# A fused linear-attention and mixture-of-experts kernel: PSUM tiles split, late logits grouped, token lists ahead of gate weights, x stored in one transfer, expert weights loaded two steps later

## The chip, the cores and the metric

The kernel runs on one core of a Trainium2 chip. The core has five engines that run side by side and meet through semaphores: TensorE (PE: matrix products; its weight loads are listed apart as PEld), VectorE (DVE), ScalarE (ACT), GpSimd (POOL) and SyncE (SP, which here only issues transfers). Transfers between the chip's memory and SBUF, the core's working memory, are carried out by 16 DMA engines. PSUM is the memory that TensorE writes; it has 8 banks of 2 KB per partition.

The metric is the device time of one execution in microseconds (us); lower is better.

## The reference, cut to what matters

```python
# linear attention: batch 4, 8 heads, 768 positions, head size 48
state = zeros((B, H, D, D))
for t in range(S):
    cur = einsum('bhd,bhe->bhde', u[None] * k[:, :, t], v[:, :, t])
    y[:, :, t] = einsum('bhd,bhde->bhe', r[:, :, t], state + cur)
    state = w[None, :, :, None] * state + einsum('bhd,bhe->bhde', k[:, :, t], v[:, :, t])
x = y as 3072 tokens of 384 numbers

# experts: 8 experts, hidden size 1024
do_compute = x @ w_skip > 0
logits = x[do_compute] @ w_gate
e_idx = argmax(logits); gate_w = softmax(logits)[e_idx]
for e in range(8):
    mask = e_idx == e
    y[mask] = gate_w[mask] * (relu(x[mask] @ w1[e]) @ w2[e])
out = x;  out[do_compute] = x[do_compute] + y
```

Each token that passes the skip score is sent to one expert, and the expert's output, weighted, is added to the token. All data are 32-bit floats.

## The kernel before, in words

**Tiles.** The 3072 tokens are 24 tiles (`NT`) of 128: two pairs of batches, 12 blocks of 64 positions (`C`) each; a tile holds the same 64 positions of the two batches of a pair, one batch on partitions 0 to 63 and one on 64 to 127. The blocks of a pair are linked by the recurrent state, so they run in order.

**The recurrence (lines 853 to 896).** Step n of the loop works on tile n+1 and finishes tile n. In order, on TensorE: `scores` (L445, keys against queries, into `ps_p`), `turn_k` (L458, keys transposed), `across` (L527, the part of the output that comes from the state), `turn_x` (L565, tile n transposed), `state` (L478, the state's update, into `ps_s[:, 0]`), the logits of tile n (`gate`, L573) and `within` (L504, the part of the output from the block itself, for which VectorE's `mask_scores`, L466 and L467, must be done). `evac` (L538) copies the finished x tile from PSUM to SBUF, and `put_x` (L552) stores it to the output tensor by two transfers of 64 rows, one per batch. Tiles 12 to 15 are stored a second time, as tiles 16 to 23 in two halves each, into rows that are rewritten later (so that a first gather may read them before).

**Logits.** Up to tile 15 the logits are made for four tiles at once: `gate_four` (L591) loads the gate's weights once per tile into a quarter of the array and multiplies by the transposed x; ScalarE copies the result (L600), and a step later `gate_back` (L604, L605) transposes it back through `ps_s[:, 1]` and copies it into `lg`. From tile 16 on, each tile has its own `gate` (L573), in which the transposed x is the loaded operand.

**Routing.** `route(g0, g1)` turns the logits of a group of tiles (`GROUPS`: 0 to 8, 8 to 16, 16 to 20, 20 to 24) into lists: for each expert, in each of two halves (j = 0 up to 128 tokens, j = 1 the rest), which token stands at which place, and its gate weight in two parts. It is a generator: each `yield` ends a portion, and `step_route` and `tick` place the portions in the steps, a `yield 4` at one of two places of a step. Its PSUM is `ps_s[:, 1]` (for the last group `ps_l`): ranks are counted by matmuls (L652 to L662), and the lists are collected by matmuls (L722, L747) of a one-hot matrix `ol` with the values `vl`: token id and the two parts of the weight (`NV3` = 3). After tile 15, L754 reduces the counts, `place(0)` derives from the lists the gather's indices `gid`, the scatter's `sid` and the weights `gate_s`, and a first indirect gather fetches the first tokens of expert 0.

**Expert weights.** `load_piece` (L108) loads a piece of 256 KB (128 partitions of 512 numbers) on the SP queue; `split_piece` splits it into a high part (ScalarE, L113) and a low part (POOL or VectorE, L114), so that products keep their precision. There are 12 pieces per expert (`NPC`). In step n, piece n-2 is loaded at the end (`FIRST_LOAD` = 2), and piece n-4 is split in the middle (`LEAD` = 2), on ScalarE ahead of the copy of the transposed keys (L460). Three buffers (`NST`) hold raw pieces.

**Order.** The program fixes the order of every engine by the order of the lines; nothing is rearranged. SP issues, per step: dm (keys and queries, L271, 512 KB, five tiles ahead), vz (values, L279, two of 96 KB, four tiles ahead), the two x stores, and the raw piece. What reads or writes a tile of PSUM or SBUF waits for what touched the tile before it where the two accesses may collide.

**The passage and the experts (lines 902 to 1040).** `first` and `second` are generators (`single`) for the first and second 128 tokens of expert 0, run in pieces (`run`) between the routing of the last group. After `place(1)` the remaining gathers go out, then `PLAN`, a string that fixes the order of portions, finishes expert 0 and begins expert 1. Experts 1 to 7 then run in `expert`: `up` (L154), `rectify`, `down` (L164), `mix` (L169), `scatter` (L172). Their weights come by `load_next` through 14 buffers.

Of the kernel before, what the change touches and what calls it, by code (L numbers as in the profile page):

```python
# [22 lines left out]
P = 128  # L23
# [26 lines left out]
NST = 3  # L50
NST2 = 14
LEAD, FIRST_LOAD = 2, 2
# [7 lines left out]
def tile_wkv_moe(  # L60
# [18 lines left out]
    ps_s = psum.tile([P, 2, 512], F32, name="ps_s")  # L79
    ps_t, ps_l = (psum.tile([P, 512], F32, name=f"ps_{c}") for c in "tl")  # L80
# [163 lines left out]
    with ExitStack() as actx:  # L244
# [51 lines left out]
        nc.vector.memset(ps_s[:, 0, : 2 * NHP * D], 0.0)  # L296
# [172 lines left out]
        def state(n):  # L469
# [5 lines left out]
            s, nxt = ps_s[:, 0, : 2 * NHP * D].rearrange("p (q f) -> p q f", q=2), sblk[(n + 1) % 2]  # L475
# [72 lines left out]
        def put_x(n, x, parts=((0, 0), (1, 1))):  # L548
            pr, i = divmod(n, NSTEP)
            for to, b in parts:  # L550
                r0 = (NB * pr + to) * S + i * C
                ins = nc.sync.dma_start(out=out[r0 : r0 + C, :], in_=x[b * C : (b + 1) * C, :])  # L552
# [32 lines left out]
        def gate_four(n):  # L585
            four = [gts.pop(n - GB + 1 + j)[1] for j in range(GB)]
# [12 lines left out]
            lt = turned_lg[n] = wk.tile([P, P], F32, tag="lt", name=f"lt{n}", bufs=1)  # L599
            nc.scalar.copy(lt, pg)  # L600

        def gate_back(n):
            pb = ps_s[:, 1, 512 - P :]
            nc.tensor.transpose(pb, turned_lg.pop(n), ident)  # L604
            nc.scalar.copy(lg[:, n - GB + 1 : n + 1, :], pb.rearrange("p (j e) -> p j e", j=GB)[:, :, : E + 1])  # L605
            seen[0] = n
# [4 lines left out]
        def route(g0, g1):  # L611
            n, late = g1 - g0, g0 >= EARLY
            rp = ps_l if g1 == NT else ps_s[:, 1]
# [25 lines left out]
            if late:  # L639
                nc.scalar.activation(df, df, AF.Exp)  # L640
# [30 lines left out]
            nc.vector.tensor_reduce(gw, df, AX.X, ALU.add)  # L671
            nc.vector.tensor_scalar(gw, gw, 1e-9, None, ALU.add)
# [12 lines left out]
            if late:  # L685
                ranks()
                nc.vector.reciprocal(gw, gw)
                nc.vector.tensor_reduce(r1, rk, AX.X, ALU.add)
                nc.vector.tensor_copy(gh, gw)
# [16 lines left out]
            yield 0  # L706
# [3 lines left out]
            if late:  # L710
                nc.vector.tensor_tensor(
                    ol, lane1[:, None, :].to_broadcast([P, n, P]), r1.unsqueeze(2).to_broadcast([P, n, P]), ALU.is_equal
                )
                nc.vector.tensor_tensor(gl, gw, gh.bitcast(F32), ALU.subtract)
                vl = small("vl", F32R, NV3 * E)
                for q, val in enumerate(vals):
                    nc.vector.tensor_tensor(
                        vl[:, :, q * E : (q + 1) * E], oh, val.to_broadcast([P, n, E]), ALU.mult
                    )
                yield 4  # L720
                for j in range(n):
                    nc.tensor.matmul(  # L722
                        part[:, :, NJ - 1, :], ol[:, j, :], vl[:, j, :], start=(j == 0), stop=(j == n - 1)
                    )
                last = lists[:, :, NJ - 1, :]
                nc.vector.tensor_tensor(last, part[:, :, NJ - 1, :], last, ALU.add)
                count()
                nc.vector.tensor_tensor(before, before, sums, ALU.add)
# [24 lines left out]
            if g1 == EARLY:  # L753
                nc.tensor.matmul(pr[:, :E], ones[:, :P], before, start=True, stop=True)  # L754
                nc.vector.scalar_tensor_tensor(
                    before, pr[:, :E], float(P), ident[:, 0:1].to_broadcast([P, E]), ALU.max, ALU.mult
                )
                place(0)
                x_in.append(gather(0, wpool, x_out, (B - 1) * S + (EARLY - NSTEP) * C))

        def place(j):
            c = slice(j * E, (j + 1) * E)
            ids = lists[:, 0, j]
            nc.vector.tensor_scalar(gid[:, c], ids, 1.0, 0.0, ALU.subtract, ALU.max)
# [22 lines left out]
        def both(g):  # L787
# [4 lines left out]
            "ph": [ps_p[:, 0], ps_s[:, 1], ps_l, ps_y[:, 1]],  # L792
            "pt": [ps_s[:, 0], ps_t],
# [59 lines left out]
        for n in range(NT - 1):  # L853
# [5 lines left out]
            if 0 < n <= EARLY and n % GB == 0:  # L859
                gate_back(n - 1)  # L860
# [57 lines left out]
        run(2)  # L918
        both(last)
        place(1)  # L920
        order = [q for e in range(E) for q in (e, E + e)][1:]

    with ExitStack() as mctx:
        w2pool = mctx.enter_context(tc.tile_pool(name="w2pool", bufs=1, reuse_waits="tile"))
        rest = iter(order)
        for _ in range(NXG - 1):
            gather(next(rest), w2pool)
# [68 lines left out]
        split_next = splitter(1, done - NPC)  # L996
# [270 lines left out]
```

## Time and profile before

| | us |
|---|---|
| three runs, without a profile | 287.99 (median), 286.94, 289.4 |
| the profiled execution, its own time | 289.88 |
| its span, first to last instruction | 288.0 |
| mean granted TensorE clock in it | 0.97 of full |

How to read the views: the page's rows in 40 digits cut the span into 40 slices of 7.2 us; a digit is the busy share in tenths (for PEclk the granted clock). The timeline has the start (us), the duration (us), the engine, the line of the kernel, the operation, output and inputs, how many instructions were merged, and in brackets how long the engine had been idle before and what released it. In the groups by line the last columns are busy time in all and mean ns of one, then the idle time before them by releaser. The table by stage has, for each stretch, its length and each engine's busy time. The list of waits has total us, times, and the longest. A releaser is inferred; where a wait is for several things, the last one by the profile is named.

### The profile page before, as it was taken

The page shows a single profiled execution, that of the slowest core. Times are in us where ns is not written, and L with a number is a line of the kernel's source. Part 1 is how long each engine was busy: PE and PEld are TensorE (multiplying, and loading weights), DVE is VectorE, ACT ScalarE, POOL GpSimd, SP SyncE. Part 2 cuts the span into 40 slices and gives each one's busy share as a digit, 9 for nine tenths or more (in the row PEclk, how much of TensorE's full clock was granted, in tenths as well). Part 3 has the DMA queues.
Part 4 walks back from the last instruction along what each step waited for, and adds up shares of the span by engine and source line. Part 5 has one row for each costly group of instructions (what it writes and reads, how often), then busy time and mean ns, then how long its engine had stood idle before and what let it go on. Part 6 is the DMA issues. An engine that isn't in the chain of part 4 may idle for free.

```text
span 288.0 us, 9596 instructions
## 1 busy us (share of the span) xinstructions
PE 260.1 (90%) x3961; PEld 233.2 (81%) x3961; DVE 194.5 (68%) x370; ACT 141.1 (49%) x318; POOL 134.6 (47%) x135
## 2 busy tenths in 40 slices
PE   7869998885979998798969999999999999999991
PEld 2658776675767787687867999999999999999991
DVE  7837598699887899973624476796847659385210
ACT  2616565565556556545325453662817447282200
POOL 8464074555545535631084384564453534445111
PEclk9979999999979999979979999999999999999997
DMA  6956879769787878432358999467774847300000
GB/s 193 256 173 170 263 226 288 215 202 280 211 256 216 251 215 254 131 92 67 100 155 256 350 327 307 165 201 238 225 241 139 252 144 242 120 5 26 17 30 22
DMA packets 28134, 54.16 MB, mean 188 GB/s; under 512 B 4727, under 2 KB 11404, under 8 KB 28080
## 3 DMA queue, kind: packets, MB, share of 16 engines
q1 hardware_dynamic: 25744, 47.99, 54.6%
q0 software_dynamic: 2048, 5.44, 5.9%
q8 instruction: 33, 0.54, 0.8%
q14 instruction: 21, 0.17, 0.2%
q10 hardware_dynamic: 288, 0.02, 0.1%
HBM read 45.64 MB, written 8.65 MB: 188 GB/s over the span
## 4 chain that ended last, share of the span: by engine, by line
PE 66%; DMA 11%; DVE 7%; issue 6%; SPq 3%; ACT 3%; POOL 3%; POOLq 0%; ACTq 0%; DVEq 0%
PE ps_p L164 10%; PE ps_y L164 10%; DMA raw<-in_w_dram 8%; PE ps_p L154 5%; PE ps_y L154 5%; PE ps_s L154 5%; PE ps_l L154 5%; PE ps_p L445 5%; PE ps_s L478 4%; PE ps_y L504 4%; DMA dm<-in_dm_dram 2%; PE ps_y L527 2%; SPq L552 2%; PE ps_l L458 2%; PE ps_t L565 1%
## 5 line engine op out<-in xcount | busy, mean ns | idle before, releaser
L114 POOL TENSOR_TENSOR lo<-raw,hi 128x512 fp32r<-128x512 f32 x43 | 57.9, 1347 | 86.7 <-ACT hi L113 79.8
L113 ACT CAST hi<-raw 128x512 fp32r<-128x512 f32 x96 | 55.2, 623 | 12.5 <-DMA raw<-in_w_dram 12.5
L114 DVE TENSOR_TENSOR lo<-raw,hi 128x512 fp32r<-128x512 f32 x53 | 46.1, 891 | 2.7 <-ACT hi L113 1.9
L433 POOL TENSOR_TENSOR kd<-dm,w_d 128x512 f32<-128x512 f32 x22 | 32.3, 1468 | 6.7 <-DMA dm<-in_dm_dram 6.7
L172 POOL DMA_INDIRECT out_dram<-xg,sid x16 | 17.2, 1075 | 36.7 <-DVE xg L169 30.2
L445 PE MATMUL ps_p<-rd,kd 64*64 64x128 f32 x768 | 30.2, 290 | 3.1 <-issue 2.2
L466 DVE COPY_PREDICATED am<-below,ps_p 128x512 f32<-128x512 int8 x24 | 17.6, 732 | 18.4 <-PE ps_p L445 18.2
L445 PEld LDWEIGHTS ps_p<-rd,kd 64*64 64x64 f32 x768 | 24.0, 144 | 4.6 <-issue 3.2
L478 PE MATMUL ps_s<-vz,kt 128*64 128x96 f32 x352 | 19.9, 256 | 5.5 <-ACT kt L460 2.9
L478 PEld LDWEIGHTS ps_s<-vz,kt 128*64 128x64 f32 x352 | 15.7, 139 | 11.2 <-ACT kt L460 4.3
L122 POOL DMA_INDIRECT xg<-out_dram,gid x16 | 17.7, 1106 | 15.1 <-DVE gate_s L768 10.3
L415 DVE TENSOR_TENSOR rd<-dm,w_d 128x512 f32<-128x512 f32 x24 | 23.1, 962 | 1.1 <-DMA dm<-in_dm_dram 1.1
L158 ACT ACTIVATE hh<-ps_p 128x464 fp32r<-128x464 f32 x7 | 3.9, 559 | 37.8 <-PE ps_p L154 20.2
L504 PE MATMUL ps_y<-vz,am 64*64 64x48 f32 x768 | 17.8, 230 | 4.2 <-issue 2.5
L504 PEld LDWEIGHTS ps_y<-vz,am 64*64 64x64 f32 x768 | 14.5, 141 | 7.2 <-issue 3.4
L409 ACT ACTIVATE rd<-rd,uw 128x128 f32<-128x128 f32 x52 | 17.9, 397 | 4.5 <-DVE rd L415 4.5
L164 PE MATMUL ps_p<-hi,hh 128*128 128x384 f32 x56 | 19.4, 347 | 0.0
L164 PE MATMUL ps_y<-hi,hh 128*104 128x384 f32 x56 | 18.9, 338 | 0.0
L164 PE MATMUL ps_p<-hi,hl 128*128 128x384 f32 x56 | 18.9, 337 | 0.0
L164 PE MATMUL ps_y<-lo,hh 128*104 128x384 f32 x56 | 18.9, 337 | 0.0
L164 PE MATMUL ps_y<-hi,hl 128*104 128x384 f32 x56 | 18.9, 337 | 0.0
L164 PE MATMUL ps_p<-lo,hh 128*128 128x384 f32 x56 | 18.8, 336 | 0.0
(247 smaller groups left out, 682.5 us busy)
## 6 DMA issues: line engine op xcount, KB each, us to landing
raw<-in_w_dram SPq DMA_DIRECT2D x96, 256.0 KB
dm<-in_dm_dram SPq DMA_DIRECT2D x24, 512.0 KB
out_dram<-xt SPq DMA_DIRECT2D x56, 96.0 KB
vz<-in_tok_dram SPq DMA_DIRECT2D x48, 96.0 KB
xg<-out_dram,gid POOLq DMA_INDIRECT x16, 6.9
out_dram<-xg,sid POOLq DMA_INDIRECT x16, 2.7
w_in<-in_wd_dram SPq DMA_DIRECT2D x1, 8.0 KB
ub_sb<-in_ub_dram ACTq DMA_DIRECT2D x1, 2.0 KB
```

Source lines behind the costliest of these rows:

```text
L113: nc.scalar.copy(hi, t)
L114: eng.tensor_tensor(lo, t, hi.bitcast(F32), ALU.subtract)
L122: ins = nc.gpsimd.indirect_dma_start(out=xg, out_offset=None, in_=out[0:rows], in_offset=bass.IndirectOffsetOnAxis(ap=gid[:, q : q + 1], a ...
L154: nc.tensor.matmul(ph, a[:, c, fs], b[:, c, :], start=(k == 0), stop=(k == 3 * NCC - 1))
L164: nc.tensor.matmul(py, a, b[:, f, :], start=(k == 0), stop=(k == 3 * NFC - 1))
L409: nc.scalar.mul(rd[:, :, 1], rd[:, :, 0], uw[:, hp : hp + 1])
L415: nc.vector.tensor_tensor(rds[n][:, :, :, 0], d[:, 0], w_d[:, n % NSUB, 0][:, :, None].to_broadcast([DR, NHP, 2, C]), ALU.mult,)
L433: (eng or nc.gpsimd).tensor_tensor(kds[n], d[:, 1], w_d[:, n % NSUB, 1][:, :, None].to_broadcast([DR, NHP, 2, C]), ALU.mult,)
L445: nc.tensor.matmul(ps_p[q * C : (q + 1) * C, a, 2 * hp * C : 2 * (hp + 1) * C], kd[h, hp, q, :], rd[h, hp, q].rearrange("p s c -> p (s c)" ...
L466: nc.vector.copy_predicated(shape(am[n % 2]), below, p[:, :, 0])
L478: nc.tensor.matmul(s[a * C : (a + 1) * C, :, hp * D : (hp + 1) * D], kt[:, hp, a, :], t[:, :, a, hp, :], start=i == 0 and hp == 0, stop=Tr ...
L504: ins = nc.tensor.matmul(ps_y[b * C : (b + 1) * C, a, hp * D : (hp + 1) * D], am[n % 2][half, a, hp * C : (hp + 1) * C], t[half, q, a, hp, :],
```

## The change

Five edits go together.

1. The two-bank PSUM tile `ps_s` becomes two tiles, `ps_s` (state) and `ps_r` (routing). In the route that ends at tile 16 the matmul that reduces the counts stands ahead of the matmuls that collect the lists.
2. `gate_four` becomes `gate_some`: tiles 16 to 19 have their logits as a group of four, tiles 20 to 22 as a group of three; only tile 23 has a gate of its own.
3. In the late routes the token ids are collected by themselves and the gather's indices follow at once (`place_ids`); the gate weights are worked out and collected after that. At the end, the gather of expert 0's second tokens goes out before the weights are there.
4. An x tile is stored by one transfer of 128 rows, two blocks of 64 rows in the output, instead of two transfers; the second copy of tiles 12 to 15 likewise, as 128 rows in one block.
5. Weight pieces are loaded two steps later (`FIRST_LOAD` = 4), through four buffers (`NST` = 4), so two more are loaded and split after the loop.

The diff, with its smaller renamings left out:

```diff
-NST = 3
+NST = 4
-LEAD, FIRST_LOAD = 2, 2
+LEAD, FIRST_LOAD = 2, 4
...
-    ps_s = psum.tile([P, 2, 512], F32, name="ps_s")
-    ps_t, ps_l = (psum.tile([P, 512], F32, name=f"ps_{c}") for c in "tl")
+    ps_s, ps_r, ps_t, ps_l = (psum.tile([P, 512], F32, name=f"ps_{c}") for c in "srtl")
...
             if FIRST <= n < EARLY:
-                for b in range(NB):
-                    put_x(EARLY + NB * (n - FIRST) + b, x, ((0, b),))
-            put_x(n, x)
-
-        def put_x(n, x, parts=((0, 0), (1, 1))):
+                r0 = (B - NB) * S + (EARLY - NSTEP) * C + (n - FIRST) * P
+                put_x(n, x, out[r0 : r0 + P, :])
             pr, i = divmod(n, NSTEP)
-            for to, b in parts:
-                r0 = (NB * pr + to) * S + i * C
-                ins = nc.sync.dma_start(out=out[r0 : r0 + C, :], in_=x[b * C : (b + 1) * C, :])
-                if n >= EARLY:
-                    for other in x_in:
-                        tc.declare_no_dep(ins.ins, other, reason="the rows are disjoint")
-                    x_out.append(ins.ins)
+            put_x(n, x, out.rearrange("(b s) c -> b s c", b=B)[NB * pr : NB * (pr + 1), i * C : (i + 1) * C, :])
+
+        def put_x(n, x, to):
+            ins = nc.sync.dma_start(out=to, in_=x)
...
-        def gate_four(n):
-            four = [gts.pop(n - GB + 1 + j)[1] for j in range(GB)]
+        def gate_some(n, k=GB):
+            four = [gts.pop(n - k + 1 + j)[1] for j in range(k)]
...
+                def collect(v0, v1):
+                    for j in range(n):
+                        nc.tensor.matmul(
+                            part[:, v0:v1, NJ - 1, :],
+                            ol[:, j, :],
+                            vl[:, j, v0 * E : v1 * E],
+                            start=(j == 0),
+                            stop=(j == n - 1),
+                        )
+                    into = lists[:, v0:v1, NJ - 1, :]
+                    nc.vector.tensor_tensor(into, part[:, v0:v1, NJ - 1, :], into, ALU.add)
+
+                value(0)
+                yield 4
+                collect(0, 1)
+                if g1 == NT:
+                    place_ids(1)
+                yield 0
+                weigh()
+                nc.vector.reciprocal(gw, gw)
+                nc.vector.tensor_copy(gh, gw)
                 nc.vector.tensor_tensor(gl, gw, gh.bitcast(F32), ALU.subtract)
...
+                value(1, 2)
+                if g1 < NT:
+                    count()
+                    nc.vector.tensor_tensor(before, before, sums, ALU.add)
                 yield 4
...
+                collect(1, NV3)
...
             yield 2 if g1 < EARLY else 4
+            if g1 == EARLY:
+                nc.tensor.matmul(pr[:, :E], ones[:, :P], before, start=True, stop=True)
             for j in range(n):
                 nc.tensor.matmul(mine, ol[:, j, :], vl[:, j, :], start=(j == 0), stop=(j == n - 1))
...
-            if n >= EARLY:
-                gate(n)
-            elif n % GB == GB - 1:
-                gate_four(n)
+            if n < TE and n % GB == GB - 1:
+                gate_some(n)
+            elif n == NT - 2:
+                gate_some(n, NT - 1 - TE)
...
         run(1)
         turn_x(NT - 1)
+        piece(done, split=True)
+        gate_back(NT - 2, NT - 1 - TE)
         run(1)
         gate(NT - 1)
...
-        run(2)
+        run(1)
+        next(last)
+        gather(E, wpool)
+        while next(last) == 0:
+            pass
+        run(1)
         both(last)
+        piece(done + 1, split=True)
+        run(1)
         place(1)
-        order = [q for e in range(E) for q in (e, E + e)][1:]
+        order = [q for e in range(E) for q in (e, E + e)][2:]
```

More of the change, by code (lines that the diff above doesn't have):

```diff
@@ L295, in tile_wkv_moe @@
         nc.gpsimd.memset(am[1], 0.0)
-        nc.vector.memset(ps_s[:, 0, : 2 * NHP * D], 0.0)
+        nc.vector.memset(ps_s[:, : 2 * NHP * D], 0.0)
         def lower(name, op):
@@ L598, in gate_four, with gate_back @@
                     )
[L599 to L605, printed above, removed]
+            lt = turned_lg[n] = wk.tile([P, P], F32, tag="lt", name=f"lt{n}", bufs=1)[: k * w]
+            nc.scalar.copy(lt, pg[: k * w])
+        def gate_back(n, k=GB):
+            m = k * P // GB
+            pb = ps_r[:, 512 - m :]
+            nc.tensor.transpose(pb, turned_lg.pop(n), ident[:m, :m])
+            nc.scalar.copy(lg[:, n - k + 1 : n + 1, :], pb.rearrange("p (j e) -> p j e", j=k)[:, :, : E + 1])
             seen[0] = n
@@ L612, in route @@
             n, late = g1 - g0, g0 >= EARLY
-            rp = ps_l if g1 == NT else ps_s[:, 1]
+            rp = ps_l if g1 == NT else ps_r
             mine = rp[:, : NV3 * NSL]
@@ L713, in route, with value @@
                 )
-                nc.vector.tensor_tensor(gl, gw, gh.bitcast(F32), ALU.subtract)
[L715 to L719, printed above, removed]
-                yield 4
[L721 to L728, printed above, removed]
+                vl = small("vl", F32R, NV3 * E)
+                def value(*qs):
+                    for q in qs:
+                        nc.vector.tensor_tensor(
+                            vl[:, :, q * E : (q + 1) * E], oh, vals[q].to_broadcast([P, n, E]), ALU.mult
+                        )
[7 more added lines that the diff above has]
+                            stop=(j == n - 1),
+                        )
+                    into = lists[:, v0:v1, NJ - 1, :]
[5 more added lines that the diff above has]
+                    place_ids(1)
+                yield 0
+                weigh()
+                nc.vector.reciprocal(gw, gw)
+                nc.vector.tensor_copy(gh, gw)
+                nc.vector.tensor_tensor(gl, gw, gh.bitcast(F32), ALU.subtract)
+                value(1, 2)
+                if g1 < NT:
+                    count()
+                    nc.vector.tensor_tensor(before, before, sums, ALU.add)
+                yield 4
+                collect(1, NV3)
                 nc.vector.tensor_scalar(over[:, g0:g1], r1, float(CAP), None, ALU.is_ge)
@@ L753, in route @@
             if g1 == EARLY:
-                nc.tensor.matmul(pr[:, :E], ones[:, :P], before, start=True, stop=True)
                 nc.vector.scalar_tensor_tensor(
@@ L757, in route, with place_ids @@
                 )
+                place_ids(0)
                 place(0)
                 x_in.append(gather(0, wpool, x_out, (B - 1) * S + (EARLY - NSTEP) * C))
+        def place_ids(j):
+            nc.vector.tensor_scalar(gid[:, j * E : (j + 1) * E], lists[:, 0, j], 1.0, 0.0, ALU.subtract, ALU.max)
         def place(j):
@@ L791, in tile_wkv_moe @@
         banks = {
-            "ph": [ps_p[:, 0], ps_s[:, 1], ps_l, ps_y[:, 1]],
-            "pt": [ps_s[:, 0], ps_t],
+            "ph": [ps_p[:, 0], ps_r, ps_l, ps_y[:, 1]],
+            "pt": [ps_s, ps_t],
             "py": [ps_p[:, 1], ps_y[:, 0]],
@@ L858, in tile_wkv_moe @@
             scores(n + 1)
-            if 0 < n <= EARLY and n % GB == 0:
+            if 0 < n <= TE and n % GB == 0:
                 gate_back(n - 1)
@@ L925, in tile_wkv_moe @@
         rest = iter(order)
-        for _ in range(NXG - 1):
+        for _ in range(NXG - 2):
             gather(next(rest), w2pool)
```

22 lines of the change are left out of this document (12 added, 10 removed).

## The prediction

> **What bounds the kernel now.** I read the page first: span, clock, transfers, chain.
>
> ```profile
> span 288.0 us, 9596 instructions
> PE 260.1 (90%) x3961; PEld 233.2 (81%) x3961; DVE 194.5 (68%) x370; ACT 141.1 (49%) x318; POOL 134.6 (47%) x135
> PEclk9979999999979999979979999999999999999997
> DMA  6956879769787878432358999467774847300000
> q1 hardware_dynamic: 25744, 47.99, 54.6%
> PE 66%; DMA 11%; DVE 7%; issue 6%; SPq 3%; ACT 3%; POOL 3%; POOLq 0%; ACTq 0%; DVEq 0%
> raw<-in_w_dram SPq DMA_DIRECT2D x96, 256.0 KB
> dm<-in_dm_dram SPq DMA_DIRECT2D x24, 512.0 KB
> out_dram<-xt SPq DMA_DIRECT2D x56, 96.0 KB
> vz<-in_tok_dram SPq DMA_DIRECT2D x48, 96.0 KB
> w_in<-in_wd_dram SPq DMA_DIRECT2D x1, 8.0 KB
> ```
>
> Three things stand there. TensorE is busy 90% of the span and carries two thirds of the chain. Its clock dips four times (the 7s at slices 3, 12, 18 and 21). And the transfers are busy mostly 7 to 9 tenths through the first 17 slices, so the early part of the kernel is nearly as much a matter of transfers as of TensorE. Next, the table by stage, whose columns after the stretch are its length, each engine's busy time, and at the end clock, DMA share and GB/s:
>
> ```profile
> 12.00:136.00 124.00, 108.30 (x2862) 90.36 (x2854) 98.00 (x184) 68.89 (x170) 59.64 (x55) 0.96 0.71 208
> 136.00:158.00 22.00, 19.05 (x103) 16.05 (x102) 9.99 (x39) 9.32 (x23) 9.33 (x9) 0.92 0.55 163
> 158.00:282.00 124.00, 123.94 (x905) 122.03 (x904) 76.37 (x119) 58.13 (x115) 56.34 (x45) 1.00 0.54 177
> ```
>
> From 158 on TensorE has no gap, and nothing of the change lies there: those 124 us stay. All must come from the 23 steps of the recurrence (12 to 136, 5.4 us a step) and the passage (136 to 158). The sum is made against this execution, 289.88 us for its span of 288.0, which is 1.9 us above the median of the three runs, 287.99.
>
> **The change part by part.** *PSUM tiles of their own, and the count's matmul moved ahead of the list's.* The timeline of step 20 shows what this removes.
>
> ```profile
> 121.16 0.72 DVE L467 COPY_PREDICATED am<-eye,ps_p 128x512 f32<-128x512 int8 x1
> 121.78 0.19 DVE L752 TENSOR_TENSOR lists<-ps_s,lists 128x48 f32<-128x48 f32 x1
> 122.02 0.17 PE L754 MATMUL ps_s<-before,ones 128*128 128x8 bf16 x1 [1.69 <-DVE lists L752]
> 122.49 0.88 PE L478 MATMUL ps_s<-vz,kt 128*64 128x96 f32 x16 [0.30 <-DVE gid L764]
> ...
> 125.35 1.99 PE L445 MATMUL ps_p<-rd,kd 64*64 64x128 f32 x32
> ...
> 131.72 1.10 PE L445 MATMUL ps_p<-rd,kd 64*64 64x128 f32 x32
> ```
>
> TensorE waits 1.69 + 0.30 us for VectorE work that it needs only because a routing read sits between (L754), and because state and routing share a tile (L478). With both gone it runs on, until within(21) needs the mask that ends at 121.9: about 2.0 us are won, not more. Then the clock: after this gap the 32 score matmuls took 1.99 us instead of 1.10. Without the dip 0.9 us more, and about 0.4 on L504 before it, by the same ratio. The Trainium skill (TensorE: Matmul & The Clock Gate, What's actually happening) has the clock fall only after an idle window of about 3.4 us. Here it fell after a gap of some 2.2 us, so the row decides; by the rule those 1.3 us would not be won.
>
> *Logits in groups.* These are the groups, a line of waits, and the step-18 row of the shared tile.
>
> ```profile
> L573 PE MATMUL ps_t<-wg_sb,xT 128*128 128x9 f32 x42 | 5.9, 261 | 0.6 <-ACT xT L567 0.6
> L591 PE MATMUL ps_t<-xT,wgp 128*32 128x128 f32 x96 | 3.5, 277 | 0.0
> L478 PE MATMUL ps_s<-vz,kt 128*64 128x96 f32 x352 | 19.9, 256 | 5.5 <-ACT kt L460 2.9 <-ACT rd L409 1.5 <-POOL w_d L326 0.8
> ACT hi L113 <- DMA raw<-in_w_dram: 12.5, 11, 2.4
> 109.94 0.88 PE L478 MATMUL ps_s<-vz,kt 128*64 128x96 f32 x16 [1.06 <-ACT rd L409]
> ```
>
> Seven gates cost 5.9 us; a group of four costs 3.5/4 = 0.9, one of three 0.7, and two transposes 0.3 each. About 3.7 us of TensorE go. Steps 18 and 21 also wait for VectorE, so I count two thirds, 2.5. The 1.06 us at 109.94 is the shared tile again, though VectorE's chain stands close behind: 0.5. The logits come no later where it counts: route (16, 20) starts in step 20 in any case, behind route (8, 16).
>
> *Token lists ahead of gate weights* works in the passage.
>
> ```profile
> 141.31 0.18 DVE L717 TENSOR_TENSOR vl<-oh,gh 128x32 fp32r<-128x32 bf16 x1
> ...
> 142.53 0.17 DVE L726 TENSOR_TENSOR lists<-ps_l,lists 128x24 f32<-128x24 f32 x1
> ...
> 143.37 0.16 DVE L768 TENSOR_TENSOR gate_s<-lists 128x8 f32<-128x8 f32 x1
> ...
> 143.96 1.02 POOL L122 DMA_INDIRECT xg<-out_dram,gid  x1 [10.30 <-DVE gate_s L768]
> ...
> 144.60 0.34 PE L216 MATMUL ps_p<-lo,hh 128*128 128x384 f32 x1
> ...
> 147.87 0.90 PE L145 MATMUL ps_t<-ident,xg 128*128 128x128 f32 x3 [2.23 <-DMA xg<-out_dram,gid]
> ...
> 149.21 0.52 PE L216 MATMUL ps_p<-hi,hh 128*128 128x384 f32 x1
> ```
>
> The gather waits for gate_s, though it needs the ids alone. Seven small weight operations of about 0.17 us leave the way to L726 (1.2 us), and the 0.9 us from L726's place to gate_s leave it too: the gather goes out about 2 us earlier, and the 2.23 us wait at 147.87 shrinks by as much. The slow stretch after it (0.52 instead of 0.34 a matmul, some ten of them) may go too, up to 1.7. The added second collect costs four matmuls and one 0.17 us addition behind the gather: nothing.
>
> *Weights later.* Two pieces leave steps 2 to 4, where nothing needs them; a fourth buffer adds no wait. ScalarE waits 12.5 us for late pieces, of which TensorE feels the 2.9 us "ACT kt" of the L478 row. One SP issue less in front of each piece (0.6 us) and two pieces fewer early: 1.2 won. Two splits move into the passage: on ScalarE and on POOL, ahead of or behind the gather in its own queue. POOL has been idle 10.3 us there, so nothing; without that cover it would be a 1.3 us split in front of the gather. Five loads instead of three stand on SP before expert 2's: 1.1 us on loads used after 158: nothing.
>
> *x in one transfer.* This is the part that decides. SP's issue falls by one per tile (0.6 us, counted above). But what the transfer becomes is not in this trace. 225 SP transfers move 96·128 + 24·128 + 56·64 + 48·64 + 128 = 22,144 rows, and the queue counts 25,744 packets: 3,600 more, 16 for each. So every transfer now closes on all 16 engines, and each has 64 or 128 rows as outermost count on both sides. The new store has 128 partitions on one side and 2 blocks of 64 rows on the other. Either it still goes over 16 engines, at no cost, or it can be cut only as both sides can be cut, in two: 2 engines of 16 then take 64 rows each, 98,304 bytes, where an engine took 8 rows. The rates, from the view of transfers at 136 to 141 (slices of 0.125 us: the two stores of the last x first, then two weight pieces):
>
> ```profile
> GB/s 82 16 0 0 0 0 0 0 0 0 0 0 160 221 197 172 37 160 221 197 160 50 115 147 131 213 279 246 311 344 213 262 279 459 360 377 279 115 49 16
> out_dram<-xt SPq DMA_DIRECT2D x2, 96.0 KB
> 12.66 1.14 SPq L552 DMA_DIRECT2D out_dram<-xt  x2
> 136.38 1.11 SPq L552 DMA_DIRECT2D out_dram<-xt  x2
> ```
>
> Stores ran at 221 GB/s at best, loads at up to 459: 13.8 or 28.7 per engine, and 7.1 or 3.4 us for the narrow store. A store that reads 64 partitions reaches just half of what a load into 128 does, which points to the half of the partitions, not to the engine; two engines on different halves would not have that limit. So I take a load's rate, 377/16 = 23.6 GB/s: 4.2 us a store. The same two engines also carry a sixteenth of each step's loads: dm 32 KB, vz 12, raw 16, in all 61,440 bytes or 2.6 us. Together 6.8 us a step, against 5.4 now.
>
> The sum on such an engine: first store at 12.7; 24 stores of 4.2 are 100.8; what is queued between them, 19 dm, 20 vz and 18 raw shares (1136 KB), 49.3; four second copies of 12 KB, 2.1. The last x lands at 165, and the gathers read x from memory. They go out at 165.2, not 143.96: 21 us later, and all behind them moves with it. At the lower end, 28.7 GB/s, the last x would land at 137 and nothing be lost; at the upper, 227. What the other parts win is TensorE's and VectorE's time in steps that now wait for the store, so it is not subtracted. 289.9 + 21 = 311; against the median run, 309. I write 310.
>
> The Trainium skill (DMA: Bandwidth & Descriptors, Why a DMA increments its semaphore by 16 and not by 1) says a transfer takes the largest number of engines up to 16 that divides the outermost count of both sides. That would be two here. No run of before shows such a transfer.
>
> **The rivals.** *Faster: the store is still spread.* For it: every SP transfer so far was. Against it: none had sides that differ. The price is then the sum of the parts: 2.0 + 1.3 + 2.5 + 0.5 + 1.2 + 2.0 + 1.7 = 11.2 us. I take a third off for waits that come in their place (masks on VectorE, late pieces): 7.5, so 282. This decides as soon as the store's share on an engine stays under about 2.5 us a step, which with 2.6 us of loads is below the present 5.4.
>
> *No change.* The store is spread, but VectorE's masks and late pieces eat what TensorE wins: 287 to 290. For it: VectorE is busy 98 of the 124 us and shows in steps 18 and 20. Against it: the passage's 2 us depend on neither.
>
> *Far slower.* Narrow at the store's own 13.8 GB/s: 24·7.1 = 170, loads at 28.7 GB/s 41, copies 3.6, start 12.7: last x at 227, so 83 us later, 373. For it: it is the only rate a store shows. Against it: half the partitions explain that rate.
>
> **How the numbers follow.** That the transfer is cut where both sides can be cut I hold likelier than not, 0.62: a split into 16 equal runs exists on one side only. Within it 0.5 for the load's rate (about 300 to 330, since the TensorE clock may dip in longer gaps) and 0.12 for the store's own. Spread: 0.30 faster, 0.08 no change. About 1% is what a measurement of this kernel can tell from none. So slower by over 1%: 0.62; within 1%: 0.08; faster: 0.30. The predicted time is that of the likeliest, 310, its own range 300 to 330. For 8 in 10 the range reaches from 279, which leaves 0.06 below, to 345, which leaves 0.12 above.
>
> **What would show it.** Right: the store of an x lands 4 us and more after its issue, the issue-to-gather wait ends on the last x, steps last 6 to 7 us with ScalarE waiting for raw and xt, and the packet count falls by less than its transfers would explain (16 for each). Wrong: steps of 4.8 to 5.2 us from tile 16 on and a first gather before 142. The single parts: no wait at the count's matmul, no 7 in slice 18, seven gates fewer, and ids ready before the weights.

## The result and the profile after

| | before | after |
|---|---|---|
| median of 4 runs each, us | 287.97 (286.94 to 289.4) | 312.78 (311.29 to 313.49) |
| ratio, 95% interval | | 1.085 (1.079 to 1.092) |
| the profiled execution: own time / span, us | 289.88 / 288.0 | 311.29 / 309.5 |
| mean granted TensorE clock in it | 0.97 | 0.94 |

The changed kernel is slower by 24.8 us; the forecast was 310, slower. Some executions of a kernel fall into a slower state at a lower clock: ratios and intervals in this document leave these out, medians and ranges hold every run. First the page of the changed kernel, with the lines that answer to those of before:

```profile
span 309.5 us, 9559 instructions
PE 260.9 (84%) x3971; PEld 233.6 (75%) x3971; DVE 183.2 (59%) x370; ACT 140.4 (45%) x315; POOL 132.0 (43%) x135
PEclk9999976997689999798996999999999999999999
DMA  7965454664455665533243799958575665600001
q1 hardware_dynamic: 24960, 47.99, 47.8%
PE 52%; DMA 31%; DVE 5%; issue 3%; ACT 3%; POOL 3%; SPq 2%; POOLq 0%; DVEq 0%; ACTq 0%
out_dram<-xt SPq DMA_DIRECT2D x28, 192.0 KB
```

TensorE is as long busy as before (260.9 against 260.1 us), so against that kernel the loss is waiting. Transfers now carry 31% of the chain instead of 11%, although the 16 engines are *less* busy: mostly 4 to 6 tenths through the first 17 slices, where before it was mostly 7 to 9. That points to few engines as the limit, not all. The queue's packets say how few: 22,144 rows as before, and 2816 packets of 4 bytes, with which each engine closes its share of a transfer. Of the 197 SP transfers 173 have 64 or 128 rows as outermost count on both sides and close on 16 engines each, 2768 packets; the 24 new stores share the other 48, two each. That is what the forecast took for likelier than not. The Trainium skill (DMA: Bandwidth & Descriptors, Why a DMA increments its semaphore by 16 and not by 1) gives two engines for an outermost count of 2 on one side; the trace agrees.

The stages (length, busy times, clock, DMA share, GB/s), the waits (total us, times, longest) and the issues of the store (duration in ns: shortest, median, longest; first and last start) of the changed kernel:

```profile
12.00:136.00 124.00, 89.46 (x2418) 74.31 (x2414) 70.99 (x141) 57.37 (x141) 46.59 (x47) 0.90 0.56 187
136.00:158.00 22.00, 18.82 (x447) 15.97 (x435) 15.94 (x46) 10.47 (x25) 7.75 (x6) 0.92 0.29 84
```

```profile
ACT hi L112 <- DMA raw<-in_w_dram: 48.0, 16, 10.1
DVE am L465 <- PE ps_p L444: 35.8, 16, 7.1
PE ps_s L477 <- ACT kt L459: 32.7, 13, 9.2
POOL kd L432 <- DMA dm<-in_dm_dram: 14.6, 5, 4.2
```

```profile
L549 SPq DMA_DIRECT2D out_dram<-xt x28: 350/577/647, 12.0 to 156.0; - x28
```

The 23 steps between the first and the last x take 144.0/23 = 6.3 us each, where before they took (136.4 - 12.7)/23 = 5.4. In the same 124 us TensorE is busy 89 us instead of 108. ScalarE waits 48.0 us for weight pieces (12.5 before), and TensorE waits 32.7 us (2.9 before) for the keys that ScalarE copies out behind such a piece. One step shows the link, in the timeline:

```profile
48.32 0.62 ACT L112 CAST hi<-raw 128x512 fp32r<-128x512 f32 x1 [10.06 <-DMA raw<-in_w_dram]
48.84 0.58 ACT L459 COPY kt<-ps_l 128x512 f32<-128x512 f32 x1
49.47 1.55 PE L477 MATMUL ps_s<-vz,kt 128*64 128x96 f32 x16 [9.20 <-ACT kt L459]
```

The piece is late, ScalarE stands still on it for 10.06 us, the copy of the keys stands behind it in ScalarE's order, and TensorE waits 9.20 us for that copy, though the piece is for expert 0, whose first product starts at 156.5, some 100 us later. After the wait the 16 matmuls take 1.55 us instead of 0.88: the clock has dropped too. Then the passage:

```profile
156.05 0.52 SPq L549 DMA_DIRECT2D out_dram<-xt  x1
...
158.53 0.62 ACT L112 CAST hi<-raw 128x512 fp32r<-128x512 f32 x1 [1.39 <-DMA raw<-in_w_dram]
159.05 0.17 ACT L603 COPY lg<-ps_r 128x27 f32<-128x27 f32 x1
...
164.22 0.17 DVE L786 TENSOR_SCALAR gid<-lists 128x8 uint32<-128x8 f32 x1
164.30 0.18 DVE L669 TENSOR_REDUCE gw<-df 128x4 f32<-128x32 f32 x1
164.66 1.02 POOL L121 DMA_INDIRECT xg<-out_dram,gid  x1 [4.17 <-DVE gw L669]
```

The last x is issued at 156.05 instead of 136.38, 19.7 us later, and the gather goes out at 164.66 instead of 143.96, 20.7 us later. So nearly all of the loss is there before the last store leaves, and nearly nothing is added behind the gather: from there to the end it takes 144.0 us before and 144.8 after. The gather itself was released by VectorE's chain for the ids, not by the store: in the packet records of the trace the last packet of that store ends at 162.8.

### The profile page after: what moved, and what is told of

Same layout as the page of the kernel before. It is cut to its first block, busy times and chain, and to the rows that moved or that the text cites. A ratio compares the mean times of both kernels' runs of the same rounds, so it can differ in the third digit from the quotient of the medians.

```text
span 309.5 us, 9559 instructions
## 1 busy us (share of the span) xinstructions
PE 260.9 (84%) x3971; PEld 233.6 (75%) x3971; DVE 183.2 (59%) x370; ACT 140.4 (45%) x315; POOL 132.0 (43%) x135
## 4 chain that ended last, share of the span: by engine, by line
PE 52%; DMA 31%; DVE 5%; issue 3%; ACT 3%; POOL 3%; SPq 2%; POOLq 0%; DVEq 0%; ACTq 0%
DMA raw<-in_w_dram 20%; DMA dm<-in_dm_dram 11%; PE ps_p L163 10%; PE ps_y L163 10%; PE ps_y L153 5%; PE ps_p L153 5%; PE ps_r L153 5%; PE ps_l L153 5%; PE ps_s L477 2%; PE ps_y L503 2%; SPq L549 2%; PE ps_t L588 2%; POOL xg L121 1%; PE ps_y L215 1%; ACT kt L459 1%
## 5 line engine op out<-in xcount | busy, mean ns | idle before, releaser
L477 PE MATMUL ps_s<-vz,kt 128*64 128x96 f32 x352 | 21.4, 269 | 33.3 <-ACT kt L459 32.7
L113 DVE TENSOR_TENSOR lo<-raw,hi 128x512 fp32r<-128x512 f32 x53 | 44.8, 867 | 2.7 <-ACT hi L112 2.3
L477 PEld LDWEIGHTS ps_s<-vz,kt 128*64 128x64 f32 x352 | 17.0, 148 | 37.5 <-ACT kt L459 35.4
L432 POOL TENSOR_TENSOR kd<-dm,w_d 128x512 f32<-128x512 f32 x22 | 29.4, 1336 | 16.4 <-DMA dm<-in_dm_dram 14.6
L444 PE MATMUL ps_p<-rd,kd 64*64 64x128 f32 x768 | 29.2, 295 | 0.2 <-ACT rd L408 0.2
L121 POOL DMA_INDIRECT xg<-out_dram,gid x16 | 18.5, 1155 | 7.9 <-DVE gw L669 4.2
L414 DVE TENSOR_TENSOR rd<-dm,w_d 128x512 f32<-128x512 f32 x24 | 19.2, 799 | 4.3 <-DMA dm<-in_dm_dram 4.3
L163 PE MATMUL ps_p<-hi,hh 128*128 128x384 f32 x56 | 19.4, 347 | 0.0
```

The source lines that it names most:

```text
L113: eng.tensor_tensor(lo, t, hi.bitcast(F32), ALU.subtract)
L121: ins = nc.gpsimd.indirect_dma_start(out=xg, out_offset=None, in_=out[0:rows], in_offset=bass.IndirectOffsetOnAxis(ap=gid[:, q : q + 1], a ...
L163: nc.tensor.matmul(py, a, b[:, f, :], start=(k == 0), stop=(k == 3 * NFC - 1))
L414: nc.vector.tensor_tensor(rds[n][:, :, :, 0], d[:, 0], w_d[:, n % NSUB, 0][:, :, None].to_broadcast([DR, NHP, 2, C]), ALU.mult,)
L432: (eng or nc.gpsimd).tensor_tensor(kds[n], d[:, 1], w_d[:, n % NSUB, 1][:, :, None].to_broadcast([DR, NHP, 2, C]), ALU.mult,)
L444: nc.tensor.matmul(ps_p[q * C : (q + 1) * C, a, 2 * hp * C : 2 * (hp + 1) * C], kd[h, hp, q, :], rd[h, hp, q].rearrange("p s c -> p (s c)" ...
```

## The experiments

All ratios are to the kernel before, run on the same chip: e1 to e4 on one, u1 to u4 on a second, u5, p1, p2 and n1 on a third. The median holds all runs, so a ratio is not always that of two medians. The letters are the names used below; the diffs are cut to the lines that matter.

| kernel | median, us | ratio | 95% interval |
|---|---|---|---|
| after | 312.78 | 1.085 | 1.079 to 1.092 |
| e2: before + the store in one transfer | 312.31 | 1.093 | 1.086 to 1.099 |
| e1: after, x in two transfers of 64 rows | 278.49 | 0.976 | 0.972 to 0.980 |
| e3: after, x in one transfer to one block | 274.84 | 0.958 | 0.952 to 0.964 |
| e4: e1, one of the two on ScalarE's queue | 276.36 | 0.963 | 0.958 to 0.968 |
| u1: e1, weights early again | 278.31 | 0.977 | 0.970 to 0.983 |
| u2: e1, single gates again | 283.27 | open (277.16 to 288.23 us) | |
| u3: e1, shared PSUM tile and count behind | 286.03 | 1.005 | 0.997 to 1.012 |
| u5: e1, count behind alone | 279.55 | 0.973 | 0.961 to 0.986 |
| u4: e1, gather late again | 278.64 | 0.973 | 0.965 to 0.982 |
| p1: before + PSUM part | 283.73 | 0.987 | 0.982 to 0.993 |
| p2: p1 + one of the two stores on ScalarE's queue | 279.30 | 0.969 | 0.950 to 0.989 |
| n1: after, the one transfer on ScalarE's queue | 305.83 | 1.065 | 1.054 to 1.077 |

**Is it the store?** The change with the store taken back, and the store alone.

```diff
 # e1: in evac, the changed kernel
-put_x(n, x, out.rearrange("(b s) c -> b s c", b=B)[NB * pr : NB * (pr + 1), i * C : (i + 1) * C, :])
+for b in range(NB):
+    r0 = (NB * pr + b) * S + i * C
+    put_x(n, x[b * C : (b + 1) * C, :], out[r0 : r0 + C, :])
 # e2: in evac, the kernel before
-put_x(n, x)
+to = out.rearrange("(b s) c -> b s c", b=B)[NB * pr : NB * (pr + 1), i * C : (i + 1) * C, :]
+put_one(n, x, to)
```

> The changed kernel with each x tile stored again by two transfers of 64 rows (the second copies of tiles 12 to 15 stay one transfer of 128 rows in one block). Theory (the store on 2 engines is the whole loss): steps fall from 6.2 us back below 5.4, ScalarE's wait for raw pieces from 48 us to under 13, and the other four parts show their gain: 282 us (278 to 286). Rival (the loss comes from loading the weights two steps later, which makes each piece late): stays at 305 to 313.

> The kernel before with one edit: the x tile is stored by one transfer into two blocks of 64 rows (second copies as before). Theory: the two engines set the pace, 6.2 to 6.8 us a step, 310 to 318 us; 2 closing packets for each of the 24 stores. Rival (weights later is the loss): 288, no change.

Both came out plainly. The store alone makes the kernel before as slow as the whole change does (1.093, and the intervals overlap); without it the rest of the change is faster than before, 0.976, so some 7 us. The rival, that the late weights are the loss, falls with both: e2 has the weights early and is slow, e1 has them late and is fast. Of the version with two stores, from the page, the waits and the stages:

```profile
PEclk9999999999999999899999999999999999999997
```

```profile
ACT hi L112 <- DMA raw<-in_w_dram: 11.1, 9, 2.5
PE ps_s L477 <- ACT kt L459: 4.4, 5, 2.2
```

```profile
12.00:130.00 118.00, 105.83 (x2854) 86.67 (x2852) 99.35 (x196) 68.91 (x170) 58.79 (x53) 0.99 0.72 220
146.00:268.00 122.00, 122.00 (x892) 120.43 (x891) 76.07 (x117) 58.10 (x115) 56.39 (x45) 1.00 0.55 177
```

The waits for pieces are back at 11.1 us and TensorE's for the keys at 4.4, the transfers are spread again (0.72 of 16 engines where the changed kernel has 0.56), and the clock dips once where before it dipped four times. The clock is a part of the loss, too: the changed kernel has TensorE busy 260.9 us, e1 with the same TensorE instructions 253.5, so some 7 of the 34.7 us between the two spans are longer work at the lower clock (0.94 against 0.99), and the rest is waiting. In the kernel with the store alone the waits for pieces stand at 42.6 us:

```profile
ACT hi L113 <- DMA raw<-in_w_dram: 42.6, 16, 5.3
```

**One transfer, or the shape of its sides?** The third kernel also stores each x by one transfer, but into 128 rows that lie together. Its output rows stand in another order, and tiles 16 to 19 share their rows with tiles 20 to 23, so it is no version to use; the bytes and the transfers are the same. The fourth keeps two transfers and lets ScalarE issue one of them.

```diff
 # e3: one block of 128 rows
+r0 = n * P if n < 14 else 2304 + (n - 14) * P if n < EARLY else 2560 + (n % 4) * P
+put_x(n, x, out[r0 : r0 + P, :])
 # e4: on top of e1
-    put_x(n, x[b * C : (b + 1) * C, :], out[r0 : r0 + C, :])
+    put_x(n, x[b * C : (b + 1) * C, :], out[r0 : r0 + C, :], nc.scalar if b else nc.sync)
```

> The changed kernel, but each x tile goes by one transfer into one block of 128 rows; the rows of the output are therefore in another order, and tiles 16 to 19 share theirs with 20 to 23. Theory: 16 closing packets per store, 8 rows on each engine, 279 to 283 us, at most 2 us under the run with two stores (one SP issue of 0.6 us less in front of each piece). Rival (one transfer of 192 KB is slow by its size, or delays what stands behind it on SP): 300 or more. A store that reads all 128 partitions should reach the rate of the loads, 20 to 29 GB/s an engine, not 13.8.

> The run with two stores, the second of them issued by ScalarE's queue right behind its copy of the tile. Theory: SP's issue is a small matter: within 1.5 us of the run with two stores, either way (SP is 0.6 us earlier with each piece; ScalarE loses some 0.5 us a step ahead of the piece's copy and the keys' copy). Rival (SP's issue time is what makes pieces late): 3 us or more faster than with two stores on SP.

With 128 rows on both sides one transfer costs nothing: 0.958, and the queue's count is again 16 for each of 197 transfers:

```profile
q1 hardware_dynamic: 25296, 47.99, 53.7%
```

22,144 + 197·16 = 25,296. So neither the single transfer nor its 192 KB are at fault, but the 2 as outermost count on the side of the memory. Both kernels gain more than was expected of one SP issue less in each step: by the medians 3.6 us in e3 and 2.1 us in e4, by the ratios 1.8% and 1.3% (the prediction had 1.2 us for it together with the pieces). That the issue alone does this is not shown, since each has another difference beside it: in e4 half of the store stands on another queue than the loads, and in e3 all 128 partitions are read at once. For the latter the packet records have a price. In each of e3's stores a row takes 65 to 66 ns of its engine (median). In the kernel before and in e1 a row of the last x takes some 106 ns. What ScalarE pays for its 24 issues in e4 does not show. Of the versions that compute the reference, e4 is the fastest by the ratio, 3.7% faster than before, and it takes 11% less time than the change as made.

**Two engines, or the queue?** In the changed kernel the pieces wait on the same queue as the narrow stores. The same transfer, issued by ScalarE, parts the two.

```diff
-put_x(n, x, out.rearrange(...)[...])
+put_x(n, x, out.rearrange(...)[...], nc.scalar)
```

> The changed kernel as it is, its single transfer of x of 128 rows issued by ScalarE's queue instead of SyncE's. If the two engines that carry the store are the limit (96 KB each a step, and their share of the loads beside it), the queue makes no difference: 1.08 to 1.09, waits for the raw piece still 40 us or more. If the loads wait only because they stand behind the store in SyncE's own queue, the waits for the raw piece fall to some 10 us and the ratio to 0.98 to 1.00.

The time lies between the two forecasts, much nearer to the first: 1.065. Its queues, its waits between 12 and 160 us, and its stores:

```profile
q1 hardware_dynamic: 21840, 43.27, 44.6%
q10 hardware_dynamic: 3408, 4.73, 4.3%
```

```profile
ACT hi L112 <- DMA raw<-in_w_dram: 17.2, 6, 6.2
PE ps_s L477 <- ACT kt L459: 20.2, 10, 5.5
ACT xt L537 <- DMA out_dram<-xt: 7.0, 6, 1.8
```

```profile
L549 ACTq DMA_DIRECT2D out_dram<-xt x24: 521/524/1487, 13.6 to 153.5; - x24
```

The waits for pieces fall by two thirds, as the queue theory asked, and yet a step still lasts 139.9/23 = 6.1 us: other waits took over, among them ScalarE waiting 7.0 us until a store has emptied an x buffer, which has nothing to do with the loads' queue. So the queue is not the limit, and standing in it with the loads adds some 2% (1.085 against 1.065).

The queue of its own also prices the store: 4.3% of 16 engines for 304.1 us are 209 us for 4.73 MB, so 22.6 GB/s for an engine and 98,304/22.6 = 4.35 us for a store. That is an upper value, since the closings and the 288 packets of before are in it. The count fits as well: 24·(128 + 2) + the 288 of before = 3408.

The packet records settle whether the two engines are full. Undisturbed, the rows of a narrow store start 61 ns apart on an engine, so 3.9 us for its 64; 2 KB packets of the loads start 80 ns apart, 4 KB ones 155. By these steps each of the two engines has, from the first x's store to the end of the last, 24·64 rows = 94 us of its own and 50 us as its sixteenth of the loads and copies. These 144 us fill 95% of the 150.8 us in the changed kernel and 98% of the 146.8 us in n1, whose own queue leaves no time without a packet under way. In the changed kernel no more than three packets are under way on all 16 engines for 61 of the 150.8 us.

**What are the other parts worth?** Each was undone alone in the version with two stores, which stands at 0.976.

```diff
 # u1
-LEAD, FIRST_LOAD = 2, 4
+LEAD, FIRST_LOAD = 2, 2
 # u2
-if n < TE and n % GB == GB - 1:
+if n >= EARLY:
+    gate(n)
+elif n % GB == GB - 1:
     gate_some(n)
 # u4
 next(last)
-gather(E, wpool)
...
 place(1)
+gather(E, wpool)
```

> The kernel with x stored by two transfers of 64 rows, and the weight loads begin at step 2 again instead of step 4 (two more pieces are loaded and split in the first steps). By the prediction's term of the change the late start of the weights is worth 1.2 us: the ratio goes from 0.976 to about 0.980. Rival: it is worth nothing, 0.976, the first steps being covered. A second rival: with the stores on all engines the pieces that come two steps earlier are useful, because the gather's wait in that kernel ends on a piece (3.75 us on the raw piece): 2 us faster, 0.969.

> The kernel with x stored by two transfers of 64 rows, and the logits of tiles 16 to 22 computed tile by tile again. By the prediction's term seven single gates cost 2.5 us more: the ratio goes from 0.976 to about 0.985, and PE's busy time between 12 and 130 us rises by about 3 to 4 us. Rival: PE waits in those steps anyway (12.00:130.00 has PE busy 105.8 of 118 us) and the ratio stays at 0.976.

> The kernel with x stored by two transfers of 64 rows, and the gather of expert 0's second tokens issued behind the last lists and weights instead of ahead of the gate weights. The prediction priced the earlier gather at about 2 us, and up to 1.7 us more for a clock dip behind the wait: the ratio goes from 0.976 to 0.983, at most 0.989, and PE waits about 2 us for the gathered tokens behind the expert's first turn. Rival: PE has enough work of expert 0's first tokens to cover it and the ratio stays at 0.976.

The late weights are worth nothing that can be measured (0.977), nor is the earlier issue of the gather (0.973). The intervals are half a per cent and more to either side, so 1.2 us for the weights can't be excluded; for the gather 2 us would be at the edge, and the 3.7 us of the forecast's upper end are out. Why the gather's issue gives so little, u4 shows by POOL's timeline and by TensorE's first transposes of these tokens (duration, first and last start):

```profile
137.19 1.02 POOL L121 DMA_INDIRECT xg<-out_dram,gid  x1
```

```profile
L144 PE MATMUL ps_t<-ident,xg x24: 250/270/328, 140.9 to 246.6; 128*128 128x128 f32 x15, 104*128 104x104 f32 x9
```

POOL issues the gather at 137.19, and TensorE, with other work until then, starts on its tokens at 140.9 after a wait of 0.3 us, where the kernel before waited 2.23. In u4 the ids are still made ahead of the gate weights; only the issue is late, and the wait is all but gone. The single gates stay open: the six runs of u2 lay between 277.16 us (granted clock 0.992) and 288.23 (0.95). The median is 5.0 us above that of u1 on the same chip and the best run 1.2 us below it, so the runs fit a price of the forecast's size as well as none.

**The PSUM part.** Undone whole (u3), undone in its order alone (u5), and added alone to the kernel before (p1), there also with half of the stores on ScalarE's queue (p2).

```diff
 # u3, on top of e1
-ps_s, ps_r, ps_t, ps_l = (psum.tile([P, 512], F32, name=f"ps_{c}") for c in "srtl")
+ps_2 = psum.tile([P, 2, 512], F32, name="ps_2")
+ps_s, ps_r = ps_2[:, 0], ps_2[:, 1]
+ps_t, ps_l = (psum.tile([P, 512], F32, name=f"ps_{c}") for c in "tl")
 # u3 and u5: in route, the count's matmul behind the lists'
-if g1 == EARLY:
-    nc.tensor.matmul(pr[:, :E], ones[:, :P], before, start=True, stop=True)
 for j in range(n):
     nc.tensor.matmul(mine, ol[:, j, :], vl[:, j, :], start=(j == 0), stop=(j == n - 1))
...
 if g1 == EARLY:
+    nc.tensor.matmul(pr[:, :E], ones[:, :P], before, start=True, stop=True)
```

> The kernel with x stored by two transfers of 64 rows, state and routing in one two-bank tile again and the count's matmul behind the lists' matmuls. By the prediction's terms 2.0 us of waits at step 20, 1.3 us of a clock dip after them and 0.5 us at step 18 come back: the ratio goes from 0.976 to about 0.989, with a wait of 1 to 2 us at the count's matmul and a slice of lower clock there. By the rule that the clock falls only behind long gaps, the waits return and the dip does not: 0.985. Rival: the wait moves to work that another wait covers, 0.976.

> The kernel with x stored by two transfers of 64 rows and state and routing in tiles of their own, but with the count's matmul behind the lists' matmuls again. It splits the loss of the run with the shared tile (ratio 1.005 against 0.976). If the order of the matmul carries it (the prediction's 2.0 us and the dip of 1.3 us): 0.988 to 1.00, with a wait of 1 to 2 us at that matmul. If the shared tile carries it, as the bigger part of 8 us would have it: 0.976 to 0.980. If the loss comes from more windows of half clock that any stop sets off, the ratio lies between and the windows are counted.

> The kernel before with the PSUM part alone: state and routing in tiles of their own, and the count's matmul ahead of the lists'. By the prediction's terms 3.8 us less: 0.987. If the part is worth what its removal cost (8 us): 0.972. Rival: it needs the grouped logits or the lists ahead beside it, and alone gives nothing, 1.00.

> The kernel before with the PSUM part, and with the second 64 rows of each x stored by ScalarE's queue. Leaves out the grouped logits, the lists ahead and the late weights. If those three parts are worth next to nothing, as two of the undone parts measured: the same as the best kernel so far, 0.96 to 0.97. By the prediction's terms they are worth 2.5, 2.0 and 1.2 us, and the ratio is 0.98.

With the shared tile the whole gain of the version with two stores is gone: 1.005 against 0.976, and 286.03 us against the 278.31 of u1 on the same chip. With the count behind and tiles of their own it is all there: 0.973. So the tiles carry this part, and with tiles of their own the order of the count's matmul carries nothing that can be measured (the forecast for it, 0.988 to 1.00, lies outside the interval). The shared tile with the count ahead was not run. TensorE's rows at that matmul agree. In the version with two stores it runs without a wait, ahead of the lists; in u5 it waits 0.4 us behind them, where the kernel before had 1.69:

```profile
108.88 0.17 PE L771 MATMUL ps_r<-before,ones 128*128 128x8 bf16 x1
108.91 1.05 PE L773 MATMUL ps_r<-vl,ol 128*128 128x48 f32 x8
```

```profile
PE ps_r L778 <- DVE lists L776: 0.4, 1, 0.4
```

Added alone to the kernel before, the part gives 0.987, which is 3.7 us; the prediction had 3.8. Taken away beside the other parts it costs 0.029, some 8 us. What the difference consists of is not settled. The page of u3 and its waits between 12 and 160 us show a lower clock in four slices and waits, one of them with no releaser in the trace:

```profile
PEclk9999999999995999886999999999999999999998
```

```profile
PE ps L479 <- ACT kt L461: 5.4, 5, 1.7
PE ps_t L566 <- issue: 3.3, 1, 3.3
PE ps L479 <- ACT rd L410: 2.5, 2, 1.6
```

The waits at the count's matmul and at the state behind it are not among them: they are 0.4 and 0.3 us. And since the profiled execution, at 288.42 us, lies 2.4 us above the median of u3, these rows show what can happen there, not what the 8 us are. The clock can be half of them at most, by an estimate: the mean granted clock is 0.975 in the runs of u3 that the ratio counts and 0.988 in those of u1, and 1.2% of 284 us are 3.5 us.

The PSUM part and half of the stores on ScalarE's queue, put on the kernel before with nothing else, give 0.969 (0.950 to 0.989). The fastest version, at 0.963, has the grouped logits, the lists ahead and the late weights besides, and lies inside that interval. So the two small edits may bring nearly all of the gain, but the interval is too wide to show it. That the old routing still costs something is seen in the timeline of p1, where TensorE waits for the gather as it did before (2.23 us there):

```profile
144.04 0.55 PE L144 MATMUL ps_t<-ident,xg 128*128 128x128 f32 x3 [1.91 <-DMA xg<-out_dram,gid]
```

## Why the prediction was right, point by point

- **The cut of the new store**, held at 0.62, decided, and it was cut in two: 48 closing packets for 24 stores. The rivals "spread" and "no change" fall with it. The mechanism that they lacked is shown from both sides: the store alone costs 9.3%, one transfer with 128 rows on both sides costs nothing, and in the changed kernel the two engines have work for 95% of the time between the first x and the last. The sign that the prediction named in the packet count stood the wrong way round: the count fell by 784, which is more than the 28·16 = 448 that 28 transfers less explain, and not less.
- **The store's time on its engine** was put at 4.2 us, at 23.6 GB/s, by the rate of a load, against 7.1 by the rate of a store. Measured: 3.9 us where nothing disturbs it, and 4.35 us at 22.6 GB/s by the queue's share, which holds the closings. So the rival "far slower" (373 us) falls. The argument for the rate, that the 221 GB/s of before come from the half of the partitions, fits the packet records of that place, the last x of the kernel before: a row took 106 ns there (median) with 16 engines on 64 partitions; it takes 65 ns in e3 with 16 engines on 128, and 65 ns on the two engines. But 20 of the 24 stores of 64 rows on ScalarE's queue in e4 have a median of 65 ns, too, so the reason is not shown.
- **The time on the two engines**, 6.8 us a step and a last x at 165, was a little too long: a step took 6.3 us, and the last x's store ended at 162.8. In the sum the 24 stores were too big, 100.8 us against 94, and the loads and copies were right, 51 us against 50. The sum had these 152 us without a pause; the records have 144 us in 150.8, so the pauses that it left out made up for most of what the stores had too much. That part is luck.
- **The place of the loss was wrong in the text.** The prediction let the gather wait for the last x, and named "the issue-to-gather wait ends on the last x" as what would show it. It ended on VectorE's ids, 1.9 us after the store was done. The backlog made itself felt in every step instead, by the pieces behind the stores, ScalarE's order and TensorE's keys: of 20.7 us at the gather, 19.7 are there when the last x is issued. The prediction named this sign too (ScalarE waiting for raw; the wait for xt, which it named beside it, does not appear in the changed kernel), without carrying the sum through it. Both ways give nearly the same time because the two engines are full either way: the last x can't land before their 144 us are done, wherever the wait for it shows. That is why the time came out near all the same: the sum gave 311 for the profiled execution, and it took 311.29; the 310 stands against a median of 312.78.
- **"What the other parts win is not subtracted"** held within the noise: the store alone gives 1.093, with all other parts 1.085, and these intervals overlap.
- **The faster rival's sum**, 7.5 us for all other parts, was right as a sum: some 7 us by the version with two stores. Its terms were not. The PSUM part at 3.8 us measured 3.7 alone, but the prediction read it off the waits at the count's matmul at step 20 (1.69 us and 0.30, and the clock behind them), and the order of that matmul measured nothing; it is the tiles, so the 3.7 next to 3.8 is luck. The late weights (1.2) measured nothing, with an interval that could hide them, and no place was seen where they are felt. Of the lists ahead (2.0, and up to 1.7) the gather's wait did go, as predicted, but its earlier issue added nothing to that, and the rest of the term was not undone by itself. SP's issue was folded into the term of the weights; the two kernels with one issue less a step gain 2 to 4 us, for which the issue was not separated from what else they change. The grouped logits (2.5) could not be told from nothing.
- **The experts, left at 124 us,** stayed: from the first transposes of expert 0's second tokens to the end it took 288.0 - 147.9 = 140.1 us before, 309.5 - 172.3 = 137.2 after and 274.8 - 137.4 = 137.4 with two stores. Of the 2.7 to 2.9 us less the slow stretch behind the old wait, 3.4 us at half clock from 147.9, can be up to 1.7, as the prediction had it; the rest is not explained.

## What to carry to other kernels

Joining two transfers into one saves an issue, but look at the outermost count of both sides before: where one side has 2 blocks, two engines of 16 carried it all here, and every transfer with a share on those two stood behind it. The sign in a profile is a queue that is less busy while more of the chain waits for it, and a count of packets that has less than 16 closings for each transfer. If the issue is what one wants to save, give it to another engine's queue: that kept 16 engines at work and won 1.3% here. With the other parts of the change the kernel is then 3.7% faster than it was, where the joined transfer made it 8.5% slower.

## What the runs showed of the hardware that was not expected

A store on two engines is not slower for each engine. By the queues' shares it ran at 22.6 GB/s (n1), where the stores of 64 rows on ScalarE's queue, spread over 16, ran at 19.4 GB/s, by the row of that queue on the page of e4 (2.38 MB in 2.8% of 16 engines for 274.4 us):

```profile
q10 hardware_dynamic: 2208, 2.38, 2.8%
```

In one place the spread store is even the slower one for its engines: a row of the last x took some 106 ns with 16 engines on 64 partitions (before, e1), and 65 ns with 16 engines on 128 (e3) or with two engines (after). Since most of the 64-row stores on ScalarE's queue in e4 take 65 ns as well, what decides is open.

TensorE's clock can stay at half for long without TensorE being idle. In the profiled execution of u2 it was at half from 114.7 to 142.0 us by the clock records of the trace; the first part of that in stages, with the clock as third last number:

```profile
110.00:114.00 4.00, 3.43 (x55) 2.95 (x46) 3.93 (x5) 1.98 (x6) 2.06 (x2) 1.00 0.44 116
114.00:118.00 4.00, 2.80 (x69) 2.70 (x69) 3.86 (x17) 1.11 (x3) 2.49 (x2) 0.59 0.21 43
118.00:122.00 4.00, 4.00 (x53) 3.26 (x47) 2.81 (x8) 1.26 (x3) 0.04 (x1) 0.50 0.44 127
122.00:126.00 4.00, 4.00 (x56) 3.66 (x56) 1.42 (x10) 1.14 (x5) 0.00 (x0) 0.50 0.00 0
126.00:130.00 4.00, 4.00 (x71) 3.84 (x71) 1.45 (x4) 0.90 (x2) 1.26 (x1) 0.50 0.44 113
```

The only gap of some length just ahead of it is 0.89 us, one of 0.67 follows at 115.5, and from 118 to 130 TensorE shows no gap at all, still at 0.50. The Trainium skill (TensorE: Matmul & The Clock Gate, What's actually happening) has the clock fall after an idle window of about 3.4 us and rise after one busy window as long; this execution shows neither. What keeps it down is open. It matters for measuring: 27 us at half clock can cost up to 13 us (an estimate, for a stretch in which TensorE is the limit), more than any part of this change but the store is worth, and another run of that same kernel has a mean clock of 0.992.
